# Start-up tables from one diagonal, and a new order of the first loads, in a fused state-space and feed-forward kernel

## The chip, the cores and the metric

The kernel runs on one core of a Trainium2 chip. The metric is device time in microseconds (us) of one execution, the lower the better; three runs of a kernel give its median. Besides that there is a profile of one execution, which records when each instruction ran on each engine: TensorE (PE for its matmuls, PEld for its weight loads), VectorE (DVE), ScalarE (ACT), GpSimd (POOL) and SyncE (SP, which only issues transfers). Names such as L234 in the profile are lines of the kernel.

## The reference: what is computed

Two steps. The first is a linear state-space layer ("SSD") over 4 sequences of 768 tokens, 8 heads, head size 32, state size 16. With `a` the decay of a token, `cum` the running sum of log a inside a chunk, and `state` carried from chunk to chunk, a chunk gives

```python
L = exp(cum[i] - cum[j]) * causal            # decay from token j to token i
y = ((C_i . B_j) * L) @ x  +  (C @ state) * exp(cum)
state = exp(sum(log a)) * state + sum_j B_j x_j^T * exp(cum_end - cum_j)
```

The second is a bilinear feed-forward layer over the 3072 tokens, 256 wide, 1536 hidden: `out = ((y @ w_a) * (y @ w_b)) @ w_out`, in float32.

## The kernel before

**Tiling.** The sequence is cut into 6 blocks of 128 tokens. A *pair* is two sequences in one block, so there are 12 pairs; pairs 0 and 1 are the two halves of block 0. The four first pairs have their tokens laid out so that a partition holds two neighbouring tokens of one of the two sequences (`r` counts those two, `bt` the sequence). The decays are products: a scan over the tokens gives the running product `Pr`, its value at the middle of the block is divided out (`rmid`), small matmuls against `selr` (the selection `sel` times `rmid`) lay the factors out by token into a bank `fps` (the *factor matmuls*, L274), and `fB` is the reciprocal of them. B and C of a pair are scaled by these factors (`bm`, `cm`, `scale_bc`), turned by PE (`transposes`, `transposes1`), copied to `BT` and `CT`, and multiplied: the scores of a pair (`scores`, L435) fill the four banks `SC[0]` to `SC[3]`, two tiles `SC0` and `SC1` of two banks each. They are multiplied by the causal table `causal` (`mask`; three of four parts on DVE, one as an ACT copy `tmp` and a POOL product), and multiplied with x (`pv_u`, `pv`, L495) to give pair outputs, which go turned into `X2T` (`evac0` for pair 0, `pv` for pair 1). `ds_mm` makes the state contribution.

**Feed-forward units.** For the first four pairs the hidden layer is cut into units (p, k2) of 256 hidden columns: four matmuls against `Wa` (`aps`), four against `Wb` (`bps`), an ACT copy of aps (`evac_a`, `asb`) and a DVE product into `hk` (`times`). The matrices are held in two halves each: `Wa[0]` and `Wb[0]` serve units k2 = 0, 1, 2, and the other halves the rest. Before the change `Wb[0]` is two tiles of a quarter each, loaded by two transfers. `Wo` is the output matrix.

**What sets the order.** The order on each engine is written out by hand; every engine works off its queue in that order and waits at an instruction until its inputs are there. Transfers are issued by SP, by ACT and by POOL (`dma_start` of `nc.sync`, `nc.scalar`, `nc.gpsimd`); the weights, which change type on the way, all go by POOL. An issue occupies the issuing engine's queue. PSUM banks other than SC are handed out by the string `BANKS`, one character for each request. Matmuls named `warmup` multiply zeros into a bank that is free.

**The start, engine by engine (before).** POOL makes `sel`, `ident`, `headm` and the two halves of `causal` with selects (L198 to L236), then issues x of pair 0, `Wa[0]`, the first quarter of `Wb`, x of pair 1; later it scales B of pair 1, makes one masked part, and issues the other quarter of `Wb` and the second halves. SP issues `a` and four loads of B and C, ACT five, before its table load. DVE derives small tables (`of_b`, `selb`, `of_h`, `indm`, `par`), scans blocks 0, 1 and 2, and takes pair 0 through. PE runs eight warm-ups, then the factor matmuls, pair 0, pair 1, and from L679 (the first up products of pair 0, which need `Wa[0]` and `X2T`) the feed-forward units. `hr`, `hs`, `hsx` on POOL give the decays between blocks; two matmuls with `indm` (`gps`) spread them into `G`, which the states need.

Of the kernel before, what the change touches and what calls it, by code (L numbers as in the profile page):

```python
# [10 lines left out]
f32 = mybir.dt.float32  # L11
# [11 lines left out]
    "01232013201321023102310231023102301230120312031201320132013201320132031023102310213203120"  # L23
    "3120310213021302130210321032103210321032103210321302130213021302130213021302130213021302"
# [4 lines left out]
def kernel(  # L29
# [45 lines left out]
    zero = big.tile([BH, Q], f32, name="zero")  # L75
    KC = d_ff // 2
    Wa = [big.tile([128, 2, KC], f16, name=f"Wa{t}") for t in range(2)]
    Wb = [
        [big.tile([128, 2, KC // 2], f16, name=f"Wb0{t}") for t in range(2)],
        big.tile([128, 2, KC], f16, name="Wb1"),  # L80
    ]
# [74 lines left out]
    def load_w(half):  # L156
        c = slice(half * KC, (half + 1) * KC)
        return [
            nc.gpsimd.dma_start(W[half], src.rearrange("(f p) e -> p f e", p=128)[:, :, c])
            for W, src in ((Wa, moe_w_a), (Wb, moe_w_b))  # L160
        ]

    def load_w0(which, part):
        W, src = ((Wa, moe_w_a), (Wb, moe_w_b))[which]
        w = (KC, KC // 2)[which]
        t_ = W[0][part] if which else W[0]
        nc.gpsimd.dma_start(t_, src.rearrange("(f p) e -> p f e", p=128)[:, :, part * w : (part + 1) * w])

    def w_of(W, k, f):
        t_, q3 = W[k // 6], k % 6 // 3  # L170
        cols = t_[q3][:, f] if isinstance(t_, list) else t_[:, f, q3 * 384 : (q3 + 1) * 384]
        return cols.rearrange("p (c kk) -> p kk c", kk=3)[:, k % 3]
# [8 lines left out]
    for p_ in range(3):  # L181
# [4 lines left out]
    load1(nc.sync, 0, 1, 0, 0, 32)  # L186
    load1(nc.scalar, 0, 1, 0, 32, 32)
    load1(nc.sync, 1, 0, 0)
    load1(nc.scalar, 1, 0, 1)
    load1(nc.sync, 1, 1, 0)  # L190
    load1(nc.scalar, 1, 1, 1)
    nc.scalar.preload_act_table_set("natural_log_exp_and_others")
    nc.vector.memset(warm.bitcast(u32), 0)
    nc.vector.memset(ident, 1.0)
    nc.vector.memset(headm, 1.0)
    nc.vector.memset(causal, 1.0)
    nc.vector.memset(zero, 0.0)
    nc.gpsimd.memset(sel, 1.0)  # L198
    nc.gpsimd.affine_select(
        out=sel,  # L200
        in_=sel,
        compare_op=ALU.is_equal,
        fill=0.0,
        base=0,
        pattern=[[-H, 2], [-2 * H, NBP], [-1, H]],
        channel_multiplier=1,
    )
    nc.gpsimd.affine_select(
        out=ident, in_=ident, compare_op=ALU.is_equal, fill=0.0, base=0, pattern=[[-1, 128]], channel_multiplier=1
    )  # L210
# [7 lines left out]
    nc.vector.tensor_copy(indm.rearrange("p (h n) -> p h n", n=N), of_h.unsqueeze(2).broadcast_to((BH, H, N)))  # L218
    for base, step in ((0, 1), (N - 1, -1)):
        nc.gpsimd.affine_select(  # L220
            out=headm,
            in_=headm,
            compare_op=ALU.is_ge,
            fill=0.0,
            base=base,
            pattern=[[-N * step, H]],
            channel_multiplier=step,
        )
    nc.vector.tensor_reduce(
        out=par, in_=headm.rearrange("p (m e) -> p e m", e=2), op=ALU.add, axis=mybir.AxisListType.X  # L230
    )
    for bt in range(2):
        v = causal[64 * bt : 64 * bt + 64]
        nc.gpsimd.affine_select(  # L234
            out=v, in_=v, compare_op=ALU.is_ge, fill=0.0, base=0, pattern=[[-1, 2], [1, Q]], channel_multiplier=-2
        )  # L236
    for bt in range(2):
        load1(nc.gpsimd, 0, 2, bt)
    load_w0(0, 0)
    load_w0(1, 0)  # L240
# [10 lines left out]
    def scan(lo, hi):  # L251
        for k in range(lo, hi):
            nc.vector.tensor_tensor_scan(Pr[:, k], a_sb[:, k], zero, 1.0, ALU.mult, ALU.add)
# [404 lines left out]
    def unit_mm(p, k2, W, kks=range(2), ps=None):  # L658
        if ps is None:
            ps = bank("aps" if W is Wa else "bps")  # L660
        for kk in kks:
# [11 lines left out]

    def units_mm(p, ks, W, order):
        pss = {k2: bank("aps" if W is Wa else "bps") for k2 in ks}
        for k2, f in order:
            for kk in range(2):
                k = 2 * k2 + kk
                nc.tensor.matmul(  # L679
                    pss[k2][:, kk * 2 * Q : (kk + 1) * 2 * Q],  # L680
                    w_of(W, k, f),
                    X2T[:, p, :, f],
                    start=(f == 0 and kk == 0),
                    stop=(f == 1),
                    skip_group_check=True,
                )
        return [pss[k2] for k2 in ks]
# [121 lines left out]
    warmup(6, SC[3])  # L809
    warmup(2, SC[3], 128)  # L810
# [3 lines left out]
    scan(1, 3)  # L814
# [7 lines left out]
    warmup(1, SC[3])  # L822
    scale_bc(0, 0, nc.vector)
    scale_bc(0, 1, nc.vector, v.rearrange("p (r b h) -> p r b h", r=2, b=NBP)[:, :, 0])
    scan(3, 4)
    tb, tcp = bank("tb"), bank("tc")
    transposes(0, [tb, tcp], lambda: warmup(1, SC[3], 128))
    nc.scalar.copy(flat(fC, 0, 1), v)
    nc.scalar.copy(flat(fC, 1, 2), v1)
    scan(4, 5)  # L830
    warmup(1, SC[3])
    warmup(2, SC[3], 128)
    scores(0)
    scale_bc(1, 0, nc.gpsimd)
    mask(product0(0, 0))
    mask(product0(0, 1))
    mask(product0(1, 1), by_pool=True)
    scale_x(0, nc.scalar)
# [302 lines left out]
```

## Time and profile before

| What | Value |
|---|---|
| Median of three runs | 122.0 us (121.74 to 122.01) |
| The profiled execution | 122.28 us, span 120.5 us from the first to the last instruction |
| PE busy | 114.9 us, 95% of the span |
| DVE, ACT, POOL busy | 87.4, 73.2, 61.7 us |
| Transfers | 13.70 MB at 114 GB/s; 62000 of 67265 packets under 512 B |
| Granted TensorE clock | full speed throughout |
| Chain that ended last | PE 83%, DMA 10%, POOL 4% of the span |

A line of a timeline gives the start in us from the span's start, how long it took, the engine, the line of the kernel, the operation, what it writes and reads, the shapes and how often; in brackets stands how long the engine had been idle and what ended that. A "q" behind an engine's name is its instruction queue issuing a transfer. A line of the chain gives start, length and what ran or was waited for.

### The profile page before, as it was taken

What the parts mean: (1) busy time and instruction counts of PE and PEld (TensorE: products, weight loads), DVE (VectorE), ACT (ScalarE), POOL (GpSimd) and SP (SyncE); (2) the same over time, 40 slices, a digit from 0 to 9 for tenths busy, and PEclk for the clock granted to TensorE, in tenths of its full rate; (3) what the DMA queues carried; (4) which work ended last, traced back from release to release, by engine and by line L of the source; (5) the groups of instructions that cost most, each with busy time, mean ns of one, the idle gap of its engine ahead of it and who ended that gap; (6) DMA issues with size and microseconds to landing.
All of it is one profiled execution on the core that took longest, in us unless ns stands there. A gap on an engine that the chain in (4) does not pass through costs nothing.

```text
span 120.5 us, 3683 instructions
## 1 busy us (share of the span) xinstructions
PE 114.9 (95%) x1436; PEld 79.0 (66%) x1436; DVE 87.4 (72%) x175; ACT 73.2 (61%) x147; POOL 61.7 (51%) x107
## 2 busy tenths in 40 slices
PE   5996999999999999999999999999999999999990
PEld 2544899888888798645476464766464684655890
DVE  5988797995979888499984999577899435847100
ACT  0485867685875667787667737645646737566220
POOL 6998998981797586299822992177200000000200
PEclk9999999999999999999999999999999999999999
DMA  2999999969959899699688964995401012010032
GB/s 61 188 152 199 184 196 163 228 116 116 102 85 124 125 129 135 118 131 161 64 147 113 217 215 110 96 161 120 143 0 44 10 41 85 0 44 5 23 107 87
DMA packets 67265, 13.70 MB, mean 114 GB/s; under 512 B 62000, under 2 KB 66864, under 8 KB 67248
## 3 DMA queue, kind: packets, MB, share of 16 engines
q1 hardware_dynamic: 62272, 9.31, 47.6%
q0 software_dynamic: 2448, 3.80, 16.6%
q10 hardware_dynamic: 2528, 0.36, 1.8%
q8 instruction: 11, 0.18, 0.6%
q14 instruction: 6, 0.05, 0.1%
HBM read 11.11 MB, written 3.15 MB: 118 GB/s over the span
## 4 chain that ended last, share of the span: by engine, by line
PE 83%; DMA 10%; POOL 4%; issue 0%; DVE 0%; ACT 0%
PE ops L768 18%; PE aps L743 18%; PE bps L743 17%; PE ops L713 8%; PE bps L664 7%; PE aps L664 6%; DMA Wa<-in_moe_w_a_dram 6%; DMA turned<-planes 4%; PE SC L420 2%; PE SC L481 2%; POOL xn L142 1%; PE SC L495 1%; PE aps L679 1%; PE SC L570 1%; POOL causal L234 1%; PE SC L435 1%
## 5 line engine op out<-in xcount | busy, mean ns | idle before, releaser
L691 ACT COPY asb<-aps 128x512 f32<-128x512 f32 x72 | 41.7, 587 | 13.8 <-PE aps L743 9.6
L753 DVE TENSOR_TENSOR hkb<-bps,asb 128x512 f16<-128x512 f32 x48 | 32.3, 689 | 13.0 <-ACT asb L691 11.9
L743 PE MATMUL aps<-XB,Wa 128*128 128x512 f16 x96 | 28.6, 379 | 0.0
L743 PE MATMUL bps<-XB,Wb 128*128 128x512 f16 x96 | 28.5, 379 | 0.0
L768 PE MATMUL ops<-Wo,hkb 128*128 128x256 f16 (+1 forms) x204 | 22.5, 267 | 0.0
L768 PEld LDWEIGHTS <-hkb 128*128 128x128 f16 x204 | 18.5, 98 | 3.1
L475 DVE TENSOR_TENSOR t<-SC,causal_q 128x512 f16<-128x512 f32 x27 | 17.2, 682 | 3.3 <-PE SC L420 3.3
L698 DVE TENSOR_TENSOR hk<-bps,asb 128x512 f16<-128x512 f32 x24 | 16.2, 684 | 3.5 <-ACT asb L691 1.2
L743 PEld LDWEIGHTS <-Wb 128*128 128x128 f16 x96 | 9.9, 103 | 10.9
L743 PEld LDWEIGHTS <-Wa 128*128 128x128 f16 x96 | 9.7, 103 | 9.1 <-issue 0.2
L782 POOL DMA_DIRECT2D out_dram<-osb x1 | 0.6, 642 | 28.0 <-ACT osb L780 28.0
L780 ACT ACTIVATE osb<-ops 128x256 f32<-128x256 f32 (+1 forms) x16 | 6.0, 377 | 14.3 <-PE ops L768 14.2
L664 PE MATMUL bps<-X2T,Wb 128*128 128x256 f16 x96 | 13.8, 273 | 0.0
L664 PE MATMUL aps<-X2T,Wa 128*128 128x256 f16 x88 | 12.7, 273 | 0.0
L713 PE MATMUL ops<-Wo,hk 128*128 128x256 f16 x96 | 11.5, 273 | 0.0
L473 POOL TENSOR_TENSOR t<-tmp,causal_q 128x512 f16<-128x512 f32 x5 | 5.8, 1160 | 8.6 <-ACT tmp L472 8.5
L664 PEld LDWEIGHTS <-Wb 128*128 128x128 f16 x96 | 9.8, 103 | 0.6
L713 PEld LDWEIGHTS <-hk 128*128 128x128 f16 x96 | 8.9, 98 | 1.4
L312 POOL TENSOR_SCALAR x<-xn 128x512 f16<-128x512 f32 x6 | 8.9, 1491 | 1.3 <-DMA xn<-in_x_dram 0.8
L319 POOL TENSOR_TENSOR planes<-cn,fC 128x256 f16<-128x256 f32 x8 | 5.0, 622 | 8.8 <-DMA cn<-in_C_dram 8.7
L664 PEld LDWEIGHTS <-Wa 128*128 128x128 f16 x88 | 8.9, 103 | 0.6
L327 POOL TENSOR_TENSOR bm<-bn,fB 128x256 f16<-128x256 f32 x11 | 6.9, 623 | 2.6 <-PE aps L664 1.1
(112 smaller groups left out, 128.7 us busy)
## 6 DMA issues: line engine op xcount, KB each, us to landing
out_dram<-osb SPq DMA_DIRECT2D x22, 128.0 KB, 1.8
xn<-in_x_dram SPq DMA_DIRECT2D x6, 256.0 KB, 4.0
cn<-in_C_dram SPq DMA_DIRECT2D x8, 128.0 KB, 4.1
bn<-in_B_dram SPq DMA_DIRECT2D x8, 128.0 KB, 4.1
xn<-in_x_dram POOLq DMA_DIRECT2D x6, 128.0 KB, 6.4
Wa<-in_moe_w_a_dram POOLq DMA_DIRECT2D x2, 384.0 KB, 7.1
Wo<-in_moe_w_out_dram POOLq DMA_DIRECT2D x2, 384.0 KB, 6.9
xn<-in_x_dram SPq DMA_DIRECT2D x4, 128.0 KB, 4.5
```

Of the source, the lines that this page charges most:

```text
L312: eng.tensor_scalar(xo, xi, XS, None, ALU.mult)
L327: eng.tensor_tensor(out=m_, in0=raw, in1=(of_pair(f, blk, bp) if factor is None else factor).unsqueeze(3).broadcast_to((128, 2, H, N)), op ...
L473: nc.gpsimd.tensor_tensor(out=o_, in0=tmp, in1=c_, op=ALU.mult)
L475: nc.vector.tensor_tensor(out=o_, in0=i_, in1=c_, op=ALU.mult)
L664: nc.tensor.matmul(ps[:, kk * 2 * Q : (kk + 1) * 2 * Q], w_of(W, k, f), X2T[:, p, :, f], start=(f == 0), stop=(f == 1), skip_group_check=True,
L691: (nc.vector.tensor_copy if on_dve else nc.scalar.copy)(asb, a_ps)
L698: nc.vector.tensor_tensor(out=s["hk"][:, 2 * k2 : 2 * k2 + 2, :].rearrange("p k q -> p (k q)"), in0=b_ps, in1=asb, op=ALU.mult)
L713: nc.tensor.matmul(o_ps[:, 0:d_model], hk[:, k, bt * Q : (bt + 1) * Q], Wo[:, k, :], start=(k == 0), stop=(k == NK - 1), skip_group_check= ...
L743: nc.tensor.matmul(t_, w_of(W, k, f), XB[:, blk - P0 // NBP, f].rearrange("p t j q -> p (t j q)"), start=(f == 0), stop=(f == 1), skip_gro ...
L753: return lambda: nc.vector.tensor_tensor(out=s["hk"][:, k], in0=ps[1], in1=asb, op=ALU.mult)
L768: nc.tensor.matmul(o_ps[:, 0:w], hk[:, k, c * Q : (c + 1) * Q], Wo[:, k, cs], start=(k == 0), stop=(k == NK - 1), skip_group_check=True,)
L780: nc.scalar.activation(out=o_sb[:, 0:w], in_=o_ps[:, 0:w], func=AF.Copy, scale=1.0 / (YS * YS))
```

## The change

- **Tables.** `ident` alone is made by a select on POOL. DVE copies `sel` out of it, scans along it for `causal_q` (which was made late by POOL), and reduces it to `headm` and `par`. `causal` is made from `causal_q` by four small matmuls that pick the even and the odd tokens, written to SC[2], and an ACT copy; `indm` is an ACT copy too.
- **Loads.** C of pair 1 goes from SP and ACT to POOL, C of pair 0 becomes one transfer per sequence again, and POOL's order is x of pair 0, half of C of pair 1, `Wa[0]`, the other half of C, `Wb[0]` in one piece, x of pair 1. The second weight halves are issued right behind the masked part of pair 0.
- **Order on PE.** Four warm-ups fewer; four first up products (`half_mm`, the first half of the contraction, units 0 and 1) stand between pair 0's first and second outputs, ahead of the transposes of pair 1's C; their other halves follow the scores of pair 1.
- **Order elsewhere.** The scan of block 2 moves behind the scaling of pair 0, the scans of blocks 4 and 5 move later, the second copy of pair 0's second outputs is on ACT, `hr`, `hs` and `hsx` stand behind the loads of pair 2 and half of `Wo` on POOL, and the gps matmuls stand behind pair 1's units. `BANKS` is a new string.

```diff
-    zero = big.tile([BH, Q], f32, name="zero")
+    zero = big.tile([128, Q], f32, name="zero")
...
-    Wb = [
-        [big.tile([128, 2, KC // 2], f16, name=f"Wb0{t}") for t in range(2)],
-        big.tile([128, 2, KC], f16, name="Wb1"),
-    ]
+    Wb = [big.tile([128, 2, KC], f16, name=f"Wb{t}") for t in range(2)]
...
     load1(nc.scalar, 0, 1, 1)
-    load1(nc.sync, 0, 1, 0, 0, 32)
-    load1(nc.scalar, 0, 1, 0, 32, 32)
+    load1(nc.sync, 0, 1, 0)
     load1(nc.sync, 1, 0, 0)
     load1(nc.scalar, 1, 0, 1)
-    load1(nc.sync, 1, 1, 0)
-    load1(nc.scalar, 1, 1, 1)
     nc.scalar.preload_act_table_set("natural_log_exp_and_others")
...
-    nc.vector.memset(headm, 1.0)
-    nc.vector.memset(causal, 1.0)
-    nc.vector.memset(zero, 0.0)
-    nc.gpsimd.memset(sel, 1.0)
-    nc.gpsimd.affine_select(
-        out=sel,
...
+    nc.vector.memset(warm.bitcast(u32), 0)
+    nc.vector.memset(zero, 0.0)
+    nc.vector.tensor_copy(sel, ident[0:BH, 0:BH].rearrange("p (b t h) -> p t b h", b=NBP, t=2))
+    nc.vector.tensor_tensor_scan(causal_q, ident, zero, 0.0, ALU.add, ALU.add)
+    nc.vector.tensor_reduce(
+        out=headm, in_=ident.rearrange("p (h n) -> p h n", n=N), op=ALU.add, axis=mybir.AxisListType.X
+    )
...
     for bt in range(2):
         load1(nc.gpsimd, 0, 2, bt)
-    load_w0(0, 0)
-    load_w0(1, 0)
+    load1(nc.gpsimd, 1, 1, 0)
+    load_w(0, 0)
+    load1(nc.gpsimd, 1, 1, 1)
+    load_w(0, 1)
     for bt in range(2):
         load1(nc.gpsimd, 1, 2, bt)
...
-    warmup(6, SC[3])
-    warmup(2, SC[3], 128)
+    warmup(4, SC[3])
+    for r in range(2):
+        for bt in range(2):
+            nc.tensor.matmul(
+                SC[2][64 * bt : 64 * bt + 64, r * Q : (r + 1) * Q],
+                ident.rearrange("p (i r) -> p r i", r=2)[:, r],
+                causal_q,
...
+    nc.scalar.copy(causal.rearrange("p r q -> p (r q)"), SC[2][:, 0 : 2 * Q])
+    nc.scalar.copy(indm.rearrange("p (h n) -> p h n", n=N), of_h.unsqueeze(2).broadcast_to((BH, H, N)))
+    warmup(1, SC[3], 128)
     scan(0, 1)
     over_mid(0, 1)
     sel_over_mid(0, 1, nc.vector)
-    scan(1, 3)
+    scan(1, 2)
...
     mask(product0(1, 1), by_pool=True)
+    load_w(1, 0)
+    w1 = load_w(1, 1)
...
     warmup(1, tcp)
+    aps = [bank("aps"), bank("aps")]
+    for k2 in range(2):
+        half_mm(0, k2, Wa, 0, aps[k2])
+    transposes1(1, SC[0])
     pv_u(0, 1, py, True)
-    transposes1(1, SC[0])
     for bt in range(2):
-        evac0(1, bt, (nc.scalar, nc.vector)[bt], py)
-    load_w0(1, 1)
-    w1 = load_w(1)
+        evac0(1, bt, nc.scalar, py)
+    scan(4, 5)
     scores(1)
-    scan(5, NBLK)
-    over_mid(2, NBLK)
     mask(product(1, 3), by_pool=True)
+    for k2 in range(2):
+        half_mm(0, k2, Wa, 1, aps[k2])
...
```

The new helper issues half of a unit's products:

```python
def half_mm(p, k2, W, f, ps):
    for kk in range(2):
        nc.tensor.matmul(
            ps[:, kk * 2 * Q : (kk + 1) * 2 * Q],
            w_of(W, 2 * k2 + kk, f),
            X2T[:, p, :, f],
            start=(f == 0 and kk == 0),
            stop=(f == 1),
            skip_group_check=True,
        )
```

Behind that, the units of pair 0, the loads of pair 2, ds, pv, the late scans, hr, hs and hsx, the second half of `Wo`, the units of pair 1 and gps follow in this order:

```python
    asb = [evac_a(aps[0])]
    scale_x(1, nc.scalar)
...
    aps.append(unit_mm(0, 2, Wa))
    asb.append(evac_a(aps[1]))
    bps = [unit_mm(0, 0, Wb), unit_mm(0, 1, Wb)]
    times(0, 0, bps[0], asb[0])
    for which in range(2):
        for bt in range(2):
            load1(nc.gpsimd, 2, which, bt)
    load_wo(0)
    ds_mm(0, 64, SC[:2])
    pv(1, DS=(0, SC[:2]), split=True)
    bps.append(unit_mm(0, 2, Wb))
...
    scan(5, NBLK)
    over_mid(2, NBLK)
    nc.gpsimd.tensor_tensor(out=hr, in0=Pr[:, 0:NG, Q - 1], in1=rmid[:, 0:NG], op=ALU.mult)
...
    load_wo(1)
...
    go((1, 0), (1, 1), (1, 2))
    gps = bank("gps")
```

## The prediction

> **What bounds the kernel now.** I read the windows first, to see which engine limits which stretch, then the chain of waits, then the timelines of the stretch that is not dense. The windows (columns: stretch, length, then busy time of PE, PEld, DVE, ACT, POOL, clock, DMA share, GB/s):
>
> ```profile
> 0.00:11.57 11.57, 8.95 (x141) 4.41 (x141) 9.03 (x32) 5.23 (x13) 10.24 (x22) 1.00 0.86 150
> 11.57:18.04 6.47, 6.47 (x118) 5.87 (x119) 5.38 (x10) 4.62 (x11) 6.00 (x11) 1.00 1.04 187
> 18.04:41.37 23.33, 23.20 (x373) 20.24 (x371) 19.62 (x42) 16.75 (x36) 17.07 (x31) 1.00 0.95 131
> 41.37:117.73 76.36, 76.33 (x808) 48.48 (x808) 53.35 (x93) 46.29 (x89) 28.36 (x45) 1.00 0.54 98
> ```
>
> From 11.57 us on PE is busy practically always, and the change leaves the work after 18.04 in its order. So the whole question is when PE gets to the sixteen matmuls of line 664 that start at 18.04 (up products of units (0,3) to (0,5) and (1,3)); call that moment M. A shift of M is, one for one, the shift of the end. The chain says what set 11.57:
>
> ```profile
> 2.53 0.41 POOL causal L234
> 2.94 1.52 POOL xn L142 x2
> 4.46 7.06 DMA Wa<-in_moe_w_a_dram
> 11.52 0.05 issue
> 11.57 1.05 PE aps L679 x8
> ```
>
> GpSimd makes tables until 2.94, issues x, then Wa at 4.46, which lands at 11.52. The timelines of PE, ACT and POOL (start, length, what):
>
> ```profile
> 1.25 2.96 PE L246 MATMUL SC<-warm 128*128 128x512 f16 x8 [1.25 <-DVE warm L193]
> 4.14 0.61 PE L274 MATMUL fps<-selr,Pr 32*64 32x16 f32 x8
> 8.72 0.31 PE L495 MATMUL py<-t,x 64*32 64x128 f16 x16
> 10.65 0.43 PE L435 MATMUL SC<-ct,bt 32*64 32x128 f16 x32 [0.53 <-DVE ct L393]
> ...
> 4.40 1.28 ACT L192 ACT_TABLE_LOAD   x1 [4.40 <-DMA bn<-in_B_dram]
> 5.99 0.84 ACT L373 ACTIVATE bt<-tb,ch 128x256 f16<-128x256 f16 x2 [0.31 <-PE tb L349]
> ...
> 11.88 1.15 POOL L473 TENSOR_TENSOR t<-tmp,causal 128x512 f16<-128x512 f32 x1 [0.56 <-ACT tmp L472]
> 13.00 0.19 POOL L861 TENSOR_TENSOR hr<-Pr,rmid 32x5 f32<-32x5 f32 x1
> 13.54 0.21 POOL L863 TENSOR_TENSOR hsx<-hs,c 32x20 f32<-32x20 f32 x1
> 13.76 1.45 POOL L142 DMA_DIRECT2D bn<-in_B_dram  x2
> 15.17 1.39 POOL L142 DMA_DIRECT2D cn<-in_C_dram  x2
> ```
>
> What to see: the scores of pair 1 (10.65) end at 11.08 (call this point S), and M is S + 6.96. The factor matmuls (4.14) come right behind the warm-ups; the ACT table load stands ahead of every ACT instruction; hsx is made ahead of the pair 2 loads.
>
> **The change part by part.**
>
> *Tables.* Off GpSimd, ahead of x, go six instructions; only one select (0.29) stays. It can begin at 1.16, 0.07 behind the ident memset as now, so x is issued at 1.40 instead of 2.89. DVE gets a 32x32 copy (0.17, the row of the 32x20 copy), a scan over 128 columns (0.41, as a scan of line 253) and a reduction of 128 elements per partition, which no row has: between 0.12 (of_b) and 0.41 (the scan), I take 0.30; the bigger zero costs what the smaller did (0.17). Two memsets (0.07, 0.27) and the 0.40 copy of indm go. DVE is then free at about 2.85, where now it waits until 2.94 for a_sb: hidden, at the upper bound 0.1 to 0.2 late, still covered by the next item.
>
> *The new wait.* The causal table is now made by four matmuls into SC[2], copied out by ACT, and the following 128-column warm-up, in the same tile, waits for that copy. Behind it in PE's queue stand the factor matmuls, for which DVE, and through it all of pair 0, waits. ACT issues three loads (0.71, 0.65, 0.71: until 2.93) instead of five, then the table load 1.28 to 4.22, then the copy. A 128x256 copy from PSUM is 0.40 (line 554); the bounds are 0.19 (128x20) and 0.59 (128x512). So the warm-up starts at 4.68 and the factors, 0.24 later as now, at 4.92 instead of 4.14. They take 0.61, or 0.42 like the second group at 5.06. The DVE reciprocal so moves from 4.80 to between 5.2 and 5.6: 0.65 later. Selr is ready at 3.75, and the moved scan of block 2 would have won 0.33 here; both now hide under the wait. Nothing between the factors and pair 0's first outputs has slack, so line 495's 8.72 becomes 9.37. The Trainium skill ("ScalarE: Activation LUTs", What ACT_TABLE_LOAD costs) puts a switch of tables at 2.66 us, drain included; the trace has 1.28, and the first activation 0.31 behind it, released by PE. By the rule the factors would start at 6.3, M would be 19.8 and the median 123.8.
>
> *Wa sooner.* Queue: x 1.40 and 2.27, half of C 2.98, Wa 3.68 (0.71 per issue), so Wa leaves 0.78 earlier. Its landing moves by at least nothing (bandwidth alone: share 0.86 in this stretch) and at most by x's 1.49 plus 0.5 for the C traffic taken off SP and ACT. It is nearest to its own issue: 10.7. The second half of C of pair 1 stands behind Wa in the same queue and lands no earlier than it, say 10.8; it used to land at 8.3. DVE's scaling of cm (0.42) and the transposes of pair 1 wait for it.
>
> *First up products inside pair 0.* Four 128x256 matmuls (0.109 each) now stand ahead of the transposes of pair 1 and of pair 0's second outputs. They need the first outputs (ACT: 9.10 + 0.65, two copies, 0.45), the second bt (0.48) and Wa. From the inputs: start at 10.25, second half 10.62, done 10.85. By C: 10.8 + 0.42 + 0.05, so the transposes start at 11.3 and end (0.22 and drain) at 11.5; the ct copy and the scores take 0.97 as now (10.11 to 11.08). S becomes 12.45, against 12.05 if only the ACT wait counted.
>
> *After S.* PE does 44 matmuls of 256 columns (4.80), the small ones of pv and ds (0.66) and gps (0.28): 5.74. Before: 0.49 of waiting, 48 such matmuls and 0.3 of small gaps, 6.96 in all. Two waits come in. X2T of pair 1 passes DVE behind times(0,0): about 0.15. And hsx: POOL's mask product ends at S + 1.95, then four loads and Wo (3.48, the rows from 13.76 to 17.24), then hr, hs, hsx (0.75): S + 6.2. PE is at the gps matmuls, their only reader, at S + 5.6 with the X2T wait included. So 0.6 more (0.1 if the five issues run at 0.60 as the shortest on SP do, 0.75 if PE does not wait for X2T). M = 12.45 + 5.74 + 0.15 + 0.6 = 18.94; with an hsx wait between its bounds, 0.4, it is 18.74. I take 18.75.
>
> *No cost, with the cover named.* Wb's half in one piece: about 12.0 to 12.6 against a need at S + 0.9 = 13.3; with S at 11.3 it would be 0.3 late. x of pair 1: 13.0 to 13.4, needed by ACT at 13.6. Output copy on ACT instead of DVE: 0.28 beside the ct copy. Bank order, the late causal_q pieces (0.5 on POOL at 24.5), scans moved behind times(0,2): beside PE's dense stretch; cover gone, each would cost at most its own 0.3 to 0.8. The second halves of the weights leave at the same 9.9 and are wanted from 18.0 on.
>
> **Sum.** M moves from 18.04 to 18.75, 0.7 us. The profiled execution took 122.28 (span 120.5 and 1.8 around it) and would take 123.0; it stands 0.28 above the median of 122.0, so 122.7 in medians.
>
> **Rivals.**
> *Nothing changes.* C and Wa land by 10.2 and hsx costs little: S = 12.05, M about 18.1. For it: the DMA share of the first stretch is 0.86, so the queues were not full all the time, and x would use the room before 3 us. 122.0.
> *Faster.* The weights come two microseconds sooner, because the queue in front of them empties that much sooner: Wa at 9.5, C just behind. It decides only once they land before 9.9. Then S hangs on the ACT wait at its lower bounds (copy 0.19, factors 0.42): 11.7, M 17.65. 121.6. Against it: Wa's own issue moves 0.78 only.
> *Wa is issued sooner but lands when it did.* The queue is bound by bandwidth (share over 1.0 from 8 us on). C at 11.6, S 13.25, M about 19.5: 123.5.
> *PE runs slow for longer.* The first eight warm-ups stream 3,328 columns in 2.96 us, 0.89 ns each, though the clock row reads 1.00; the three at 7.19 take 0.82 for 1,536. Full speed begins only at about 4.9, behind 3.6 us without a hole. Now PE would stand idle from 3.6 to 4.7. Slow until 8 us: 0.2 on the factors, 0.4 on the two warm-ups and 0.2 each on the transposes and scores of pair 0; S = 13.1 at most, M 19.4: 123.4. The Trainium skill ("TensorE: Matmul & The Clock Gate", Part 1) says that the clock doubles only after about 3.4 us of sustained work in a free-running window; the trace agrees (1.25 to 4.9), and no run here shows whether a window two thirds full is enough.
>
> **How the numbers follow.** A measurement of this kernel can tell about 0.3% (0.37 us). Likeliest case (122.4 to 123.1) 0.44; nothing changes 0.19; faster 0.16; Wa not sooner 0.10; slow PE 0.11. So slower 0.65, same 0.19, faster 0.16. Predicted 122.7; the likeliest case alone spans 122.4 to 123.1, the range takes in most of the others: 121.5 to 123.7.
>
> **What would show it.** Right: the causal copy on ACT at 4.2 and PE idle before it; factors at 4.9; half products near 10.3 to 10.8, then a wait for cm from DMA cn; scores of pair 1 at about 12.1; gps waiting for POOL hsx; the sixteen matmuls at 18.7. Wrong: factors before 4.5, Wa landed before 9.9, hsx ready before PE, or a later part of the trace that is not shifted by the same amount.

## The result, and the profile after

| | Before | After |
|---|---|---|
| Median, same chip (6 runs each) | 122.09 us (121.74 to 122.79) | 125.41 us (124.78 to 125.84) |
| Ratio, after to before | | 1.026, 95% interval 1.022 to 1.030 |
| The profiled execution | 122.28 us, span 120.5 | 125.7 us, span 124.0 |
| M, start of the sixteen products (timeline) | 17.88 us | 21.38 us |

The kernel became slower, as forecast, but by 3.3 us where 0.7 was predicted, and 125.41 lies outside the range of 121.5 to 123.7. M moved by 3.50 us, the time of the profiled execution by 3.42: the loss lies ahead of M, and behind M both spans have 102.6 us left. The prediction reads M as 18.04 from the chain; the timeline's 17.88 is the same moment, and the table uses timelines for both kernels. (A ratio here leaves out executions more than 1.5% above the fastest of their kernel; where a kernel spreads more widely than that, the median over all of its executions is given beside it.)

The windows of the kernel after (length, then busy time of PE, PEld, DVE, ACT, POOL, clock, DMA share, GB/s), from the start, from the end of pair 1's scores to M, and two behind M that are cut as long as those of the kernel before:

```profile
0.00:11.57 11.57, 9.11 (x88) 3.89 (x88) 7.55 (x26) 4.58 (x11) 8.74 (x16) 1.00 0.84 165
13.74:21.38 7.64, 6.16 (x113) 5.18 (x113) 6.06 (x13) 4.69 (x9) 5.90 (x10) 1.00 0.84 154
21.38:44.71 23.33, 23.33 (x380) 20.51 (x384) 19.48 (x41) 16.96 (x37) 17.33 (x32) 1.00 0.90 125
44.71:121.07 76.36, 76.30 (x808) 48.41 (x806) 53.48 (x94) 46.27 (x90) 27.62 (x42) 1.00 0.53 96
```

The last two stretches hold nearly the same matmuls as in the kernel before (380 and 808, there 373 and 808). In the first, PE counts 9.11 us busy with 88 matmuls, where it did 141 in 8.95: the same engine time buys less. In the second it is idle for 1.48 of 7.64 us. The timelines of ACT and PE (start, length, what; in brackets the idle time and what ended it) name both, and the wait at the start:

```profile
2.98 1.28 ACT L177 ACT_TABLE_LOAD   x1 [2.98 <-issue]
4.28 0.37 ACT L780 CAST causal<-SC 128x256 f16<-128x256 f32 x1
```

```profile
4.70 0.26 PE L210 MATMUL SC<-warm 128*128 128x128 f16 x1 [1.06 <-ACT causal L780]
4.89 0.61 PE L238 MATMUL fps<-selr,Pr 32*64 32x16 f32 x8
10.95 0.41 PE L459 MATMUL py<-t,x 64*32 64x128 f16 x16
11.29 0.61 PE L210 MATMUL tc<-warm 128*128 128x512 f16 x1
12.05 0.61 PE L624 MATMUL aps<-X2T,Wa 128*128 128x256 f16 x4
12.50 0.27 PE L350 MATMUL SC<-ident,cm 128*128 128x128 f16 x2
13.31 0.43 PE L399 MATMUL SC<-ct,bt 32*64 32x128 f16 x32 [0.30 <-DVE ct L357]
16.25 0.29 PE L638 MATMUL bps<-X2T,Wb 128*128 128x256 f16 x1
18.01 0.51 PE L638 MATMUL bps<-X2T,Wb 128*128 128x256 f16 x3 [1.47 <-issue]
21.07 0.29 PE L873 MATMUL gps<-hsx,c 32*64 32x20 f32 x4
21.38 1.91 PE L638 MATMUL aps<-X2T,Wa 128*128 128x256 f16 x16
```

In the kernel before, to compare:

```profile
8.96 0.39 PE L246 MATMUL tc<-warm 128*128 128x512 f16 x1
17.88 1.91 PE L664 MATMUL aps<-X2T,Wa 128*128 128x256 f16 x16
```

Three things are to be seen. PE waits 1.06 us for the causal copy, so the factors start at 4.89. A full warm-up still takes 0.61 us at 11.29, while the kernel before had it in 0.39 at 8.96: PE runs at half speed for most of the head. The traces also record the granted clock, but only from its first change on (the windows read 1.00 up to there): the first record is the step to full speed, at 12.10 us in this trace and at 4.84 in that of the kernel before. So the "full speed throughout" of the table of the kernel before doesn't hold for its first 4.84 us. The points of full speed below come from these records. And between the first and the second Wb product of unit 2, at 16.5, PE stands still for 1.47 us, "issue": nothing that the profile shows holds it. The transfers of that time hold one thing that stands out (the transfer view of 15 to 16 us: queue and kind, packets, MB, share):

```profile
q0 software_dynamic: 134, 0.19, 107.7%
q8 instruction: 1, 0.02, 6.0%
```

One packet of 16 KB brings instructions, amid 134 packets of the queue that moves the second weight halves; it starts at 15.80 and ends at 16.76, and PE goes on at 18.01. In the kernel before the corresponding packet starts at 11.26 and there is no hole.

### The profile page after: what moved, and what is told of

Its sections match the earlier page's. It is cut to its first block, busy times and chain, and to the rows that moved or that the text cites. A ratio compares the mean times of both kernels' runs of the same rounds, so it can differ in the third digit from the quotient of the medians.

```text
span 124.0 us, 3671 instructions
## 1 busy us (share of the span) xinstructions
PE 116.6 (94%) x1434; PEld 79.1 (64%) x1434; DVE 87.3 (70%) x174; ACT 73.9 (60%) x150; POOL 60.3 (49%) x100
## 3 DMA queue, kind: packets, MB, share of 16 engines
q1 hardware_dynamic: 62000, 9.28, 45.8%
## 4 chain that ended last, share of the span: by engine, by line
PE 92%; ACTq 2%; ACT 2%; issue 2%; DVE 0%
PE ops L727 17%; PE aps L702 17%; PE bps L702 17%; PE ops L672 9%; PE bps L638 9%; PE aps L638 8%; PE SC L384 2%; PE tc L210 2%; PE SC L445 2%; ACTq L139 2%; PE SC L210 2%; PE SC L399 1%; ACT L177 1%; PE aps L624 1%; PE fps L238 1%
## 5 line engine op out<-in xcount | busy, mean ns | idle before, releaser
L439 DVE TENSOR_TENSOR t<-SC,causal 128x512 f16<-128x512 f32 x12 | 7.6, 684 | 1.1 <-PE SC L399 1.0
```

Source lines behind the costliest of these rows:

```text
L439: nc.vector.tensor_tensor(out=o_, in0=i_, in1=c_, op=ALU.mult)
```

## The experiments

Times of a kernel are compared with runs of the kernel before on the same chip, whose median was 122.65, 122.86, 123.02 and 123.21 us in the four sets. So the 122.0 known at the time of the prediction lies at the low end of what that kernel does. The first theory was: the wait for ACT, and a PE that stays slow because it does less in its first 3 us, make the loss. Its rivals: the loads and the new order make it; the late instruction packet, held up by weight traffic, makes part of it; or the point of full speed is free from run to run and proves nothing.

**1. The hole ahead of the factors filled with zeros.** In the kernel after:

```diff
     nc.scalar.copy(indm...)
+    warmup(2, SC[1])
+    warmup(1, SC[1], 128)
     warmup(1, SC[3], 128)
```

> The changed kernel, with PE kept busy in the hole between the causal matmuls (3.6 us) and the ACT copy (4.7): two 512-column warm-ups and a 128-column one in the other SC tile, which waits for nothing. The wait itself stays. Theory A, the slow PE comes from the hole: the factor matmuls still start at about 4.9, full speed (a 512-column warm-up in about 0.22 instead of 0.43) begins near 5 instead of near 12, pair 0's first outputs come at 9.4 to 9.6 instead of 10.95, and the time falls by 1.2 to 1.6, to about 124.0; if the 1.47 us gap of PE at 16.5 goes as well, to 122.6. Rival B, the slow PE has nothing to do with the hole: first outputs at 10.95 and 125.4.

Ten executions lay between 122.8 and 126.23, median 125.26 (kernel before 122.65); those counted give 1.006 (1.000 to 1.012). Six of the ten stand between 125.15 and 126.23, four between 122.8 and 124.22. The one profiled (123.93) shows the same factors at 4.89 and the step to full speed inside the three warm-ups at 8.91 (1.18 us, between the 1.46 of slow ones and 0.82 of fast ones). So PE was busy from 1.4 us on, and full speed came only at 9.68 us. A filled hole alone does not bring it early, and one kernel gives two groups of times.

**2. No wait for ACT.** In the kernel after, the two warm-ups that shared a tile with the causal copy go to SC[1]:

```diff
-    warmup(1, SC[3], 128)
+    warmup(1, SC[1], 128)
     scan(0, 1)
...
-    warmup(1, SC[3])
+    warmup(1, SC[1])
     v1 = factors_mm(1, 2, bank("fps"))
```

> The changed kernel, with the two warm-ups around the first factor matmuls moved to the other SC tile, so that nothing on PE waits for ACT's copy of the causal table. Theory A (the wait costs 0.75 by itself and another 1.5 by the slow clock that its hole brings): factors at 3.8 to 4.0, no hole, full speed from about 5, pair 0's first outputs at 8.5 to 8.8, scores of pair 1 at about 11.0 to 11.4 (C of pair 1 lands at 9.9), and 122.0 to 123.4, by whether the 1.47 us gap stays. Rival C, the loads hold pair 1 anyway: the scores of pair 1 stay near 13.3 and the time falls by less than 0.5.

Factors at 3.79, first outputs at 9.85, M 19.57, median 123.92, ratio 1.012 (1.008 to 1.016), against 1.026 for the whole change. The factors came 1.10 us sooner, so did the first outputs (10.95 to 9.85), and M by 1.81. The difference to 1.10 is the hole, which shrank from 1.47 to 0.77. The rival that the loads hold pair 1 falls: its scores came 1.10 sooner too (13.31 to 12.21). PE was still at half speed when the warm-up of 9.28 took 0.63.

**3. A hole in the kernel before.**

```diff
-    warmup(6, SC[3])
-    warmup(2, SC[3], 128)
+    warmup(3, SC[3])
```

> The kernel before, with three warm-ups of 512 columns at the start instead of six and none of the two of 128 columns: PE stops at 2.5 and waits for DVE until 3.8; nothing else differs. Theory A (PE runs at half speed until it has worked 3.4 to 3.6 us without a hole): half speed until 8 us or later, pair 0's first outputs at 9.5 to 10.2 instead of 8.72, scores of pair 1 near 12, and 122.8 to 123.6. Rival B (no such effect): factors 0.3 earlier, Wa's landing at 11.5 still decides, 122.0.

Median 124.36, ratio 1.012 (1.007 to 1.016). First outputs at 10.16, half speed until then, M 19.92. So in the old kernel, with nothing else changed, fewer warm-ups cost 1.7 us by the median, though the factors came at 3.79, 0.35 sooner. At first this looked like the proof that early work sets the clock; the twelfth kernel took away much of it. The instruction packet came at 14.50 here, and PE stood 0.88 us ahead of Wb products. The profile names a DVE product for this wait, but in the kernel before the same Wb products start before that DVE product ends, so they don't need it.

**4. The second weight halves later.** In the kernel after, both issues move from POOL's masked part of pair 0 to behind that of pair 1 (to 15.63 and 16.36 us from 10.85 and 11.58).

```diff
-    load_w(1, 0)
-    w1 = load_w(1, 1)
     scale_x(0, nc.scalar)
...
     mask(product(1, 3), by_pool=True)
+    load_w(1, 0)
+    w1 = load_w(1, 1)
```

> The changed kernel, with the second halves of Wa and Wb issued behind POOL's masked part of pair 1 (about 15.7) instead of behind that of pair 0 (10.85). Theory D: the 1.47 us gap of PE at 16.5 is a late fetch of PE's own instructions (a 16384-byte packet on the instruction queue started at 15.8, while the weights' packets of 12.3 to 13.5 took up to 1.5 us each instead of 0.14). Without the weights in the queues at that time the fetch starts near 13.7 and the gap is gone; the weights, landing at 21, may cost some of it again near 20. Rival E: the gap comes from something else in PE's stream and stays at 1.47.

Two executions took 125.44 and 127.95 us, too few for a verdict on the time; the longer one is profiled. Its head is that of the kernel after to 0.01 us (factors 4.89, scores of pair 1 13.31). The instruction packet starts at 13.26, the only packet between 13 and 14 us, and the hole is gone: the Wb products run through.

```profile
16.25 0.62 PE L638 MATMUL bps<-X2T,Wb 128*128 128x256 f16 x4
21.40 0.29 PE L873 MATMUL gps<-hsx,c 32*64 32x20 f32 x4 [1.86 <-POOL hsx L857]
```

The gain is given back, because the two issues now stand ahead of hsx on POOL. (Behind that wait the granted clock is at half from 22.14 to 25.55 us, so this execution is longer still.) But the hole goes with the weight traffic: this much is shown.

**5. No wait, and as much early work as before.** The second kernel, with one full warm-up more, so that PE works from 1.39 to 4.21.

```diff
+    warmup(1, SC[1])
     warmup(1, SC[1], 128)
     scan(0, 1)
```

> The changed kernel without the wait for ACT and with 640 more warm-up columns, so that PE works from 1.4 to about 4.2 us much as the kernel before does (1.25 to 4.14). If the lost time is the wait plus a PE that stays slow for lack of early work, full speed comes at about 5 us, pair 0's first outputs at 8.7 to 9.0, the scores of pair 1 at 11.1 to 11.4, M at 17.9 to 18.5, and the time is within 0.6 us of the kernel before. If the loads and the new order cost as well, the scores of pair 1 start later than 11.8 although PE is at full speed, and the kernel stays 1 us or more slower. If full speed comes at a point that changes from run to run whatever PE did, the times spread over 2 us or more and the profile may show slow matmuls to 8 us.

Median 124.46, ratio 1.012 (1.006 to 1.018). Not as the first theory had it: half speed until 9.78, first outputs 10.05, scores 12.32, M 19.24.

**6. hsx sooner**, on top of 5: scan of block 5, hr, hs and hsx between pair 2's loads of B and of C; on DVE that scan so comes ahead of two products of pair 0.

```diff
+    scan(5, NBLK)
+    over_mid(2, NBLK)
+    nc.gpsimd.tensor_tensor(out=hr, ...)
...
     for bt in range(2):
         load1(nc.gpsimd, 2, 1, bt)
     load_wo(0)
```

> The run before, with the scan of block 5, hr, hs and hsx ahead of pair 2's loads of C and of Wo. If the wait for hsx is what is left once PE is early, gps waits 0.3 to 0.6 less than in the run before and M comes that much sooner: 0.3 to 0.6 us faster than that run. If the instruction fetch or the units are what PE waits for there, the same time as that run.

Median 124.1, ratio 1.010 (1.004 to 1.017): not told apart from 5. In the profiled execution the wait for hsx is gone, and the hole is 1.59 us.

**7. The second half of Wb later**, on top of 6: it is issued behind the masked part of pair 1.

```diff
     load_w(1, 0)
-    w1 = load_w(1, 1)
...
     mask(product(1, 3), by_pool=True)
+    w1 = load_w(1, 1)
```

> The run before, with the second half of Wb issued behind the masked part of pair 1. If the late instruction fetch of PE is held up by the second weight halves, the fetch starts within 0.5 us of the start of pair 1's scores plus 0.5, no hole of 0.5 us or more stands ahead of the Wb products of pair 0, and the time is 0.3 to 0.8 us below the run before. If the hole has another cause, it stays.

Median 124.4, ratio 1.014 (1.009 to 1.020). The instruction packet starts at 13.12 instead of 14.93 and the hole is 0.58 instead of 1.59 (the profile names an ACT copy there that had ended 0.24 earlier); the time is no better. Half of the traffic moved away shortens the hole and doesn't take it away: a miss for the size expected.

These three and the next share every instruction up to the scores of pair 0. Yet the warm-ups behind those differ. PE in kernel 5, then in kernel 7:

```profile
8.23 1.46 PE L210 MATMUL tc<-warm 128*128 128x512 f16 x3
9.49 0.42 PE L350 MATMUL tb<-ident,bm 128*128 128x128 f16 x2
```

```profile
8.24 0.82 PE L210 MATMUL tc<-warm 128*128 128x512 f16 x3
8.89 0.28 PE L350 MATMUL tb<-ident,bm 128*128 128x128 f16 x2
```

Kernel 7 went to full speed at 8.19, kernel 5 at 9.78, kernel 6 at 11.52, kernel 8 at 11.71, on the same head. The point of full speed isn't a property of the kernel alone.

**8. Transposes ahead of the products**, on top of 5, as in the kernel before:

```diff
+    transposes1(1, SC[0])
+    pv_u(0, 1, py, True)
     for k2 in range(2):
         half_mm(0, k2, Wa, 0, aps[k2])
-    transposes1(1, SC[0])
-    pv_u(0, 1, py, True)
```

> The first of these four, with pair 1's transposes and pair 0's second outputs ahead of the first up products, as in the kernel before. If the new order on PE delays the scores of pair 1, they start 0.3 to 0.9 us sooner after pair 0's first outputs than the 2.3 us of the changed kernel (1.93 in the kernel before), and the time is 0.2 to 0.6 us below that of the first. If the products only fill time in which PE waits for C, both times agree within 0.3 us.

Median 123.31, 1.15 below kernel 5, ratio 1.006 (1.003 to 1.010). The gain is more than the 0.2 to 0.6 expected. From pair 0's first outputs to pair 1's scores it takes 1.99 us instead of 2.27, at half speed nearly all the way. The instruction packet starts at 11.38 and there is no hole; instead gps waits 0.48 us for hsx at 18.98.

**9. Causal matmuls behind the first factors**, in the kernel after: the zeros are written first, six full and two short warm-ups follow as before the change, and the causal matmuls and copy take the place of the warm-up between the two groups of factors (the ACT copy of indm moves further back as well).

```diff
-    warmup(4, SC[3])
+    warmup(6, SC[3])
+    warmup(2, SC[3], 128)
...
     nc.vector.reciprocal(flat(fB, 0, 1), v)
-    warmup(1, SC[3])
+    for r in range(2):
+        for bt in range(2):
+            nc.tensor.matmul(SC[2]..., causal_q, ...)
+    nc.scalar.copy(causal..., SC[2][:, 0 : 2 * Q])
```

> The changed kernel with one part altered: the zeros for the warm-ups are written first, six full and two short warm-ups stand ahead of the factors as in the kernel before, and the four causal matmuls and their copy by ACT follow the first factors, so nothing waits for ACT and no half-width matmul stands in the early work. If full-width work in the first 3 us decides when PE goes to full speed, this kernel does so at about 5 us like the kernel before, pair 0's first outputs come at 8.6 to 9.0 and the time is 121.8 to 123.0. If the point is free from run to run, slow matmuls may go on to 8 us or beyond as in the four kernels before, and the time is 123.5 to 124.5.

**10.** The same with the transposes first (edit of 8). **11.** That with hsx sooner (edit of 6).

> The run before, with pair 1's transposes and pair 0's second outputs ahead of the first up products. If the order of the products is worth what the fourth kernel of the last set showed, 0.8 to 1.2 us faster than the run before, and no hole ahead of the Wb products; else the same time as that run. With full speed at about 5 us: pair 1's scores at 10.6 to 11.0, M at 17.5 to 18.0, some 121.5 to 122.3.

> The run before, with the scan of block 5, hr, hs and hsx ahead of pair 2's loads of C and of Wo. If the wait of gps for hsx is real there, 0.3 to 0.5 us faster than the run before; if something else takes its place (the instruction fetch), the same.

Medians 124.6, 124.03 and 123.27; ratios 1.012 (1.007 to 1.017), 1.014 (1.008 to 1.020) and 1.004 (1.000 to 1.008). With the old warm-ups up to 4.13, kernel 9 still ran at half speed to 10.36, and its hole, 1.21 us, stands between the last two of the small ds matmuls. Kernels 9 and 10 are not told apart by their ratios, so the 0.8 to 1.2 us expected of kernel 10 is not shown. In kernel 11 PE waits 0.90 us for the scaled C of pair 1 ahead of the transposes at 11.25. Kernel 10 is the most telling look at the clock. Its PE timeline:

```profile
4.13 0.46 PE L238 MATMUL fps<-selr,Pr 32*64 32x16 f32 x8
5.52 0.29 PE L313 MATMUL tb<-ident,bm 128*128 128x128 f16 x2 [0.34 <-DVE bm L291]
6.44 0.28 PE L313 MATMUL tc<-ident,cm 128*128 128x128 f16 x2 [0.42 <-DVE cm L291]
7.63 1.44 PE L210 MATMUL tc<-warm 128*128 128x512 f16 x3
```

Full speed from 4.27 us on; then two waits of 0.34 and 0.42; and at 7.63 the warm-ups are at half speed again. The granted clock shows this fall: it is at half from 7.68 to 11.10 us, a mean of 0.61 from 8 to 12. So going fast early made PE wait for DVE. That the waits lost the clock is not shown: the kernel after kept full speed over its hole of 1.47 us.

**12. The kernel before, unchanged, a second look.**

> The kernel before, unchanged, for a second look at the point where PE goes to full speed. If early work alone decides, it is 4.9 us again, and pair 0's first outputs start at 8.7. If the point is free from run to run, it lies between 4.9 and 8.5, and the time moves with it by half of the warm-ups that run slow, up to 1.5 us.

```profile
9.31 0.39 PE L386 MATMUL tb<-ident,bm 128*128 128x128 f16 x2
10.06 0.30 PE L495 MATMUL py<-t,x 64*32 64x128 f16 x16
11.99 0.43 PE L435 MATMUL SC<-ct,bt 32*64 32x128 f16 x32 [0.54 <-DVE ct L393]
15.14 0.29 PE L891 MATMUL gps<-hsx,c 32*64 32x20 f32 x4
18.66 1.58 PE L664 MATMUL aps<-X2T,Wa 128*128 128x256 f16 x13
```

Half speed until 9.54, where the first look had full speed at 4.84; first outputs at 10.06 instead of 8.72, M at 18.66 instead of 17.88; this execution took 123.25 (median of eight 122.89), the first 122.28. So the trace from which the prediction was made had an early step, which the next trace of the same kernel has not, and 0.97 us between two traces can come with no change at all.

**13. The kernel after, unchanged, a second look.**

> The changed kernel, unchanged, for a second look. If the point where PE goes to full speed is free from run to run here too, it lies anywhere between 8 and 12.5 us and pair 0's first outputs start between 10.0 and 11.0; if the changed head alone sets it, they start at 10.95 again. If the late instruction fetch is a regular part of the loss, a hole of 0.5 us or more stands again ahead of the Wb products of pair 0 or close to them; if it was chance, M is some 1.4 us sooner than 21.4. Time 124.5 to 126.

Median 125.19 (four runs, 124.73 to 125.69), ratio 1.019 (1.013 to 1.026). Factors 4.89, full speed at 10.74, scores 13.14, M 21.26, and the hole is 1.53 us, at the same matmul:

```profile
17.90 0.51 PE L638 MATMUL bps<-X2T,Wb 128*128 128x256 f16 x3 [1.53 <-issue]
```

With kernel 15 below, all three traces of this order and head have the hole.

**14. The kernel after with the transposes first, nothing else** (edit of 8).

> The changed kernel with one part undone: pair 1's transposes and pair 0's second outputs ahead of the first up products. If the order of the products costs what the pairs of kernels so far gave (0.6 to 1.1 us), this kernel is that much faster than the changed one: 124.3 to 125.0, with no hole from the instruction fetch. If only the combination with an early head gives it, 125.0 to 125.8.

Median 124.0 against 125.19 of the unchanged kernel on the same chip, 1.19 faster, a little more than forecast; ratio to the kernel before 1.010 (1.005 to 1.016) against 1.019 (1.013 to 1.026), intervals that just overlap. First outputs at 10.95 as in the kernel after; scores at 12.71 instead of 13.31; the instruction packet at 12.15, no hole; M 19.64. Its PE and its POOL show the forecast wait:

```profile
12.71 0.43 PE L399 MATMUL SC<-ct,bt 32*64 32x128 f16 x32
19.41 0.29 PE L873 MATMUL gps<-hsx,c 32*64 32x20 f32 x4 [0.46 <-POOL hsx L857]
19.64 1.60 PE L638 MATMUL aps<-X2T,Wa 128*128 128x256 f16 x13
```

```profile
15.05 1.44 POOL L139 DMA_DIRECT2D bn<-in_B_dram  x2
16.46 1.39 POOL L139 DMA_DIRECT2D cn<-in_C_dram  x2
17.81 0.77 POOL L163 DMA_DIRECT2D Wo<-in_moe_w_out_dram  x1
18.55 0.26 POOL L855 TENSOR_TENSOR hr<-Pr,rmid 32x5 f32<-32x5 f32 x1
19.15 0.21 POOL L857 TENSOR_TENSOR hsx<-hs,c 32x20 f32<-32x20 f32 x1
```

**15. The kernel after with hsx sooner, nothing else** (edit of 6).

> The changed kernel with one part undone: the scan of block 5, hr, hs and hsx ahead of pair 2's loads of C and of Wo. The prediction held 0.4 to 0.6 us for this wait; the trace of the changed kernel shows none, because the hole from the instruction fetch hides it. If that is so, this kernel takes the time of the changed one within 0.3 us.

Median 125.33, the same as the unchanged kernel (125.19); the hole is 1.40. As expected: a wait behind a hole is worth nothing until the hole goes.

**16. Kernel 11 with both halves of pair 1's C ahead of Wa.**

```diff
     load1(nc.gpsimd, 1, 1, 0)
-    load_w(0, 0)
     load1(nc.gpsimd, 1, 1, 1)
+    load_w(0, 0)
```

> The third kernel of the last set (causal matmuls behind the first factors, transposes first, hsx early), with both halves of C of pair 1 issued ahead of Wa. If the wait of PE for the scaled C of pair 1 (0.90 in that kernel's trace) is what is left against the kernel before, this kernel is 0.3 to 0.9 us faster than that one and about equal to or faster than the kernel before (ratio 0.993 to 1.001). If Wa, now issued 0.7 later, takes its place, the same as that kernel (1.004).

Median 123.36, ratio 1.004 (1.001 to 1.008), like kernel 11. Wa, issued later, did not become a wait, and the gain expected did not come. PE went fast at 4.31, waited 0.34 and 0.49 for DVE, and was slow again from 7.72 to 11.13. No kernel of these beats the kernel before.

## Why the prediction was wrong

The prediction had the sign and the wait for ACT right and missed most of the size. M was to move by 0.71 us and moved by 3.50. Of the 2.79 missed, 1.29 lies ahead of S, the end of pair 1's scores (13.74 against 12.45), and 1.50 behind it. Two steps failed: the sum behind S had no place for PE standing still without instructions, and the sum's base was one trace with an early step to full speed.

The second look at the kernel before, in which PE went to full speed late, is the nearest in clock to the kernel after. Points in us, from PE's timelines; full speed from the clock records:

| | Full speed | Factors | First outputs | Scores of pair 1 | M | Execution |
|---|---|---|---|---|---|---|
| Before, first look | 4.84 | 4.14 | 8.72 | 10.65 | 17.88 | 122.28 |
| Before, second look | 9.54 | 4.14 | 10.06 | 11.99 | 18.66 | 123.25 |
| After | 12.10 | 4.89 | 10.95 | 13.31 | 21.38 | 125.7 |
| After, second look | 10.74 | 4.89 | 10.88 | 13.14 | 21.26 | 125.57 |
| After, transposes first | 11.39 | 4.90 | 10.95 | 12.71 | 19.64 | 123.98 |

M moved 3.50 us between the two first looks: 0.78 for the base, whose clock differs (second row against first), 0.89 for the head (first outputs, 10.06 to 10.95), 0.43 between first outputs and scores (1.93 to 2.36), and 1.40 behind the scores (6.67 to 8.07), where the hole of 1.47 lies. Of these four the prediction had the second and about the third; the first and the last were in none of its terms.

**Tables: right.** x is issued at 1.42 (1.40 predicted), the scan takes 0.41, headm's reduction 0.25, and DVE still waits 0.21 for a_sb behind them.

**The new wait: right.** Factors at 4.89 (4.92), the copy 0.37 (0.40); against the second look at the kernel before, the first outputs moved by 0.89 against 0.65 predicted, 0.75 of it the factors. Kernel 2 gives the price in the whole, with the part of the hole that went too: without the wait the ratio falls from 1.026 (1.019 in the later set) to 1.012. The 2.66 us that the Trainium skill ("ScalarE: Activation LUTs", What ACT_TABLE_LOAD costs) gives a switch of tables do not appear: the load takes 1.28 and the copy starts 0.02 behind it. By the measurement there is no drain here, at the first table load of the program, which had no activation ahead of it.

**Wa sooner: wrong, without consequence.** Wa landed at 9.59 (10.7 predicted) and the second half of C at 9.86 (10.8): the queue in front had emptied sooner, the condition of the rival "Faster". But nothing waited for them any more.

**First up products inside pair 0: the size about right, the reason wrong.** S was to come 0.72 later than the head alone makes it; it comes 0.43 later than in the second look at the kernel before. Not C holds the transposes, but X2T: the products stand in PE's queue waiting for ACT's copies of the first outputs (they start at 12.05; the second look names that copy, with 0.25 us), and the transposes, whose input is there at 11.32, stand behind them. Kernel 14 prices it: 0.60 at the scores.

**After S: the failed step.** The sum took 5.74 of work and two small waits. The wait for hsx is there, 0.46 to 0.48 in kernels 1, 8, 10 and 14 against 0.4 taken; in the kernel after it is hidden under the hole. The hole is what the sum lacked: 1.47, 1.53 and 1.40 us in three looks at this order (the kernel after twice, and kernel 15). Of the second weight halves the prediction said that they leave at the same 9.9 and cost nothing, since they are wanted only from 18.0 on. They left at 10.85 and 11.58, and what they held up was not their own reader but PE's instructions.

What is shown: the hole goes when the weight traffic is moved away (kernel 4) and when the transposes stand first (8, 10, 11, 14; 0.17 left in 16); and it comes with a late instruction packet: packets that start between 11.17 and 12.6 leave no hole or 0.17, those at 13.08 to 13.26 leave none to 0.58 (kernels 1, 4, 5, 7), those at 13.99 to 15.80 leave 0.77 to 1.59 (2, 3, 6, 9, 13, 15 and the kernel after). Two readings tie the hole to the packet. It stands at one place of PE's stream: in all ten traces that have one, 449 instruction records of PE come before it, 223 of them matmuls, whatever comes next: products with Wb in most, a ds matmul in kernels 9 and 16. And in all ten PE goes on 1.24 to 1.47 us behind the packet's end. The copies and products that the profile names in kernels 3, 6 and 7 are thus not the cause.

The packet's delay has two parts, by kernels 4 and 14, which share the head of the kernel after up to the first outputs at 10.95. With the transposes first the packet starts at 12.15. With the products first and the weights moved away it starts at 13.26, though no packet at all moves between 12 and 13 us. With both the new order and the weights it starts at 15.80. So the order sets it back by 1.11 us and the weights by another 2.54. What stays argued is that PE asks for the block when it reaches a certain instruction, and that the products let it get there after the first weight packets: when the request is made, no trace shows. The new order isn't needed for a hole (kernel 3 has it with the old one) nor enough for one (kernel 1, with the order and the weights of the kernel after, has its packet at 13.19 and none); kernels 5 and 6, alike up to there but for the clock, give 13.08 and 14.93, so chance has a part in it. The Trainium skill ("Runtime: NRT & Kernel Launch", Instruction fetch mechanics) says that instructions come in blocks of 16 KiB by a queue of their own and that this is mostly hidden. The block size agrees with the packet (16,384 bytes); here it was not hidden.

**The sum's base, and the rival of the slow PE.** This is the other failed step. The sum was made against one execution as if it stood for the kernel. In it full speed came at 4.84, in the next look at 9.54, with pair 1's scores 1.34 later; that is about the 1.29 by which S was missed. The rival had chance 0.11 and 123.4; its mechanism did show in the trace (half speed to 12.10), and its S of 13.1 at most is nearer to 13.74 than the 12.45 of the sum. But the kernel before is slow as well in its second look, and beside it the head of the kernel after is longer by only 0.14 us on top of the wait for ACT. So the traces don't show that the change itself makes PE slow. It may do so on average, if the kernel before catches an early step now and then (its executions reach down to 121.56) and the kernel after doesn't (124.73 at least in ten executions); how often is open, as one profiled execution per run doesn't tell. The Trainium skill ("TensorE: Matmul & The Clock Gate", Part 1) has a free-running window of 3.4 us, so that the step varies with where the window lies when a kernel starts. The runs agree with the length: kernels 5 to 8, on one head, step between 8.19 and 11.71, a spread of about one such window, and kernels 10 and 16 hold full speed for 3.41 us and then half speed for 3.41. It also says that the point varies by half a microsecond; here it is 4.7 us in the kernel before (4.84 and 9.54). Why the step comes so late is open: in kernel 8 the profile counts PE busy without a break from 1.47 to 11.71 us, three such windows, before the step comes.

By medians, the undone parts together account for most of the loss. Against the ratio of 1.026 or 1.019 for the whole change, transposes first alone gives 1.010; no wait alone 1.012; no wait, transposes first and the hsx chain sooner, with the old warm-ups back, 1.004 (kernel 11). What is left of the change, tables on DVE and earlier loads, then buys nothing that can be measured. Each such edit also moves the instruction packet, so these parts can't be added up. Why the earlier loads gain nothing there was not taken apart; kernel 16 only shows that the order of C and Wa isn't it.

## What to carry to other kernels

Look at the base twice before summing against it: the spread of a kernel's own executions, and what in the trace could have been luck, belong to the base as much as its terms do. A transfer that is early enough for its own reader can still delay another, so ask what shares the queues with it. When work is moved ahead in an engine's queue, ask which of its inputs comes last and what ready work now stands behind it. And read the instruction packets in the transfer view: a large transfer issued shortly before an engine needs its next block of instructions can stop it where no data dependence would.

## What the runs showed of the hardware that was not expected

- PE's step to full speed lay at 4.84 and 9.54 us in two executions of one kernel, and at 8.19, 9.78, 11.52 and 11.71 in four kernels with one head. The row of the granted clock reads 1.00 up to its first record, so it doesn't show the slow start; the lengths of the warm-ups do (0.61 against 0.39 for 512 columns).
- Full speed was lost again in kernels 10 and 16 after 3.41 us, and came back after another 3.41. A stretch of the recorded clock that ends in a change lasts a whole multiple of 3.41 us in every trace that has one (3.41 to 116.05). What decides it stays open: kernel 10 had waits of 0.34 and 0.42 us, while the kernel after kept full speed over 1.47.
- PE stood still for up to 1.59 us while a 16 KB packet of instructions came late among weight packets, always behind the 449th instruction record of PE and until 1.24 to 1.47 us after the packet's end; with that traffic moved away the packet came at 13.26 and PE did not stop.
- An activation-table load of 1.28 us was followed by an ACT copy 0.02 us behind it.
